# Moving the products K S and Q S of the next chunk behind the transposes of the tokens

## The chip, the cores and the metric

The kernel runs on one core of one Trainium2 chip. The metric is device time in microseconds (us) of one execution; six runs of the kernel before gave a median of 648.7 us (648.18 to 649.58). The engines are called PE (TensorE, the matrix products), DVE (VectorE), ACT (ScalarE), POOL (GpSimd) and SP (SyncE, which here only issues transfers).

## The reference

Two things are computed one after the other. First a delta-rule attention for 4 batches x 8 heads, 768 tokens, head size 48, then a feed-forward layer on its output (3072 tokens x 384, hidden width 2048), all in float32:

```python
k_n = k / (norm(k) + 1e-6)
for t in range(S):
    y[t]  = q[t] @ state                       # read before the update
    v_old = k_n[t] @ state
    state = state + beta[t] * outer(k_n[t], v[t] - v_old)
out = gelu(y_tokens @ w_in) @ w_out
```

## The kernel before

**Chunks.** The 768 tokens are cut into 12 chunks of 64. For a chunk c the loop over tokens becomes products: Gram blocks of the keys (`grams`), a triangular inverse, products with the state (`against_state`, L605: `K S` and `Q S`, 64 small products for each of the two units, a unit being two batches x 8 heads), the subtraction of the values (`subtract`, L626: L633 and L635 on DVE, a copy on ACT, L634), `solve` (L642), `outputs` (L696: `use`, the new state L684, the tokens x L694) and `turns` (L718: six 128x128 transposes of the tokens into the layer's layout, then one copy by ACT into `xT`). Chunks are joined in pairs for the triangular inverse: `eliminate_steps` (L431) makes 30 pairs of small DVE instructions (L455, L457) and four wide 32x32-block transposes on DVE (L443, L466, L470), among them `back(0)` (L466), which writes the tile `XM` that the first join products read.

**The layer.** From chunk 2 on both layers of the feed-forward part are done with seven products in place of eight (Winograd's form of Strassen's method). The first layer (`part_of_layer`, L836) is done in two blocks b = 0, 1; each block is eleven groups of eight 128x128 products in the order P1, P5, P6, P2, R22, R11, P7, P3, R12, P4, R21. Three of them are tied to DVE: P6 is followed on DVE by L869 and L898, and P7 may write the same bank only after both; P7 is followed by L877, which reads the block C22 out of the bank that P4 goes on writing, so **P4 waits for L877**. L888 reads the bank of P3 and R12 (tag `sq`). The second layer (`two`, L913) is seven groups of 16 products, 128x192 outputs: n = 1, 5, 2, 6, 4, 7, 3; the last one, n = 3, goes to `psV2`, and L951 reads it on DVE.

**Windows.** The program is a list of steps with due times in units of a chunk; the steps are traced in order of time. In what follows *window w* is the stretch from w to w + 1: PE does the layer of chunk w - 1, and between its groups the small products of chunk w. In an odd window they are: K S and Q S at w + 0.367, `solve` with the masked Gram (`queries`) at w + 0.59, `outputs` at w + 0.72, `turns` at w + 0.93. An even window also has the two Gram products and the three join steps of a pair, and K S and Q S at w + 0.465. Each run of small products is chained by `together` (L577), which fixes the order within the run. The elimination of a pair begins in the last third of an even window and fills the odd window after it.

**Who orders what.** DVE executes exactly in the order of the due times. For PE, ACT, POOL and SP a planner chooses the order by readiness, with the traced order as priority, except where a chain (`together`, `behind`, `keep`) fixes it.

**Banks.** PSUM holds two double banks with the tag `dn` (small products, `psX` of `turns`, `psV2`), two banks `mlp`, and one each with the tags `z` and `sq`. `psK` of the two units takes both `dn` tiles.

**Transposed queries.** `turned_q` (L363, instruction L365) makes `Qt` of chunk c on DVE from the tile `Qb`, which `load_blocks` (L123, issues at L134 on SP, 16 a chunk) fills. All chunks share `Qb` and `Qt`: `Qb` of chunk c can be loaded once `turned_q` of c - 1 has read it. Values: `load_v` (issues at L96) fills `V`, four tiles for two chunks, so the tiles of chunk c come free when `subtract` of chunk c - 2 has read them; POOL then scales `V` (L337).

Of the kernel before, what the change touches and what calls it, by code (L numbers as in the profile page):

```python
# [16 lines left out]
def kernel(  # L17
# [33 lines left out]
    NC = S // C  # L51
    NP = H // 2
    NA = B // 2
# [15 lines left out]
    def dn(name):  # L69
        return ps.tile([128, 2, 512], F32, tag="dn", name=name)  # L70

    def sq(name, *shape):
        return small[0].tile([128, *shape], F32, tag="sq", name=name)
# [17 lines left out]
    tiles = {}  # L91
# [513 lines left out]
    def against_state(us):  # L605

        for u in us:
            u.W = wk.tile([128, H, D], F32, tag="W", name="W")
            u.y = None
            if u.c == 0:  # L610
                nc.gpsimd.tensor_tensor(u.W, u.V,
                                        ng[:, u.a].unsqueeze(2).to_broadcast([128, H, D]),
                                        op=ALU.mult)
                continue
            u.psK = dn("psK")[:, :, 0:2 * NP * D].rearrange("q r (x j d) -> q x r j d", x=2, d=D)
            for x in range(2):
                for j in range(NP):
                    for r, p in QUADS:
                        rows = slice(r * C, r * C + D)
                        to = HALF[p ^ (j % 2)] if x and u.c > 1 else HALF[p]  # L620
                        nc.tensor.matmul(u.psK[to, x, r, j, :], lhsT=(u.Qt if x else u.Kt)[rows, p, j, :],  # L621
                                         rhs=St[rows, u.a, p ^ r, j, :], start=True, stop=True)
        if us[0].c != 2:
            subtract(us)

    def subtract(us):  # L626
# [100 lines left out]

    def state_steps(c, first=(), second=()):
        us = [tiles[c, a] for a in range(NA)]
        return [(together, (against_state, us), *first), (together, (solve, us), *second),  # L730
                (outputs, us), (together, (turns, us))]


    FH = NF // 2
# [1 line left out]
    DH = DM // 2  # L736
# [47 lines left out]
    W2 = {}  # L784
# [128 lines left out]
    def two(c, n):  # L913
        if n == 1:
            W2["X"] = ps.tile([128, 2, DH], F32, tag="mlp", name="psX2")
            W2["o"] = [wk.tile([128, DM], F32, tag="o_sb", name="o_sb") for a in range(NA)]
            product(W2["X"][:, 0], A[0][0], B11, True)
        elif n == 5:
            W2["Z"] = small[0].tile([128, DH], F32, tag="z", name="psZ2")
            product(W2["Z"], W2["S"], T[1], True)  # L920
            W2["p1"] = more[0].tile([128, DH], F32, tag="p1", name="p1")
            nc.scalar.copy(W2["p1"], W2["X"][:, 0])
        elif n == 6:
            W2["Y"] = ps.tile([128, 1, DH], F32, tag="mlp", name="psY2")
            product(W2["Y"][:, 0], A[0][0], T[2], True)
        elif n == 2:
            product(W2["X"][:, 0], A[0][1], B21, False)
        elif n == 7:
            product(W2["Y"][:, 0], A[1][0], T[3], False)
        elif n == 4:  # L930
            product(W2["X"][:, 1], A[1][1], T[4], True)
        else:
            W2["V"] = dn("psV2")[:, 0, 0:DH]
            product(W2["V"], A[0][1], B22, True)

    def read2(c, n):
# [47 lines left out]
    def at(first, last, steps):  # L984

        total, done, timed = sum(s[0] for s in steps), 0.0, []
        for w, *step in steps:
            timed.append((first + (last - first) * (done + 0.5 * w) / total, step))
            done += w
        return timed  # L990
# [120 lines left out]
    def state_at(c, *times, first=(), second=()):  # L1111

        steps = state_steps(c, first, second)
        if len(times) > len(steps):
            steps = steps[:-1] + [(turn, tiles[c, a]) for a in range(NA)]
        return [(t, step) for t, step in zip(times, steps) if t is not None]
# [27 lines left out]
    for c in range(4, NC):  # L1144
        us = [tiles[c, a] for a in range(NA)]
        t = {4: 1.8, 5: 2.1}.get(c, c - 2.9)
        plan += [at(t, t + 0.01, [(1.0, load_blocks, c, "Kb", k)])]
        t = 3.2 if c == 4 else c - (0.72 if c % 2 == 0 else 0.9)
        plan += [at(t, t + 0.01, [(1.0, load_blocks, c, "Qb", q)])]
        t = c - (2.1 if c % 2 == 0 else 2.62) if c > 5 else {4: 2.1, 5: 2.74}[c]  # L1150
        plan += [at(t, t + 0.01, [(1.0, load_k, c, "Kn")])]
        plan += [at(c - 0.4, c - 0.39, [(1.0, load_k, c, "Kp")])]
        t = {4: 2.7262, 5: 2.955}.get(c, c - (1.77 if c % 2 == 0 else 2.57))
        plan += [at(t, t + 0.0005, [(1.0, turned_k, u) for u in us])]
        t = c + (-0.12 if c % 2 == 0 else 0.23)
        plan += [at(t, t + 0.01, [(1.0, turned_q, u) for u in us])]
    def gram(c):
        return [(grams, [tiles[c, a] for a in range(NA)])] if c < NC else []

    def query(c):  # L1160
        return [(queries, [tiles[c, a] for a in range(NA)])]
# [13 lines left out]
    for c in range(2, NC):  # L1175
        for b in range(NB):
            t = c + 1.06 + 0.2576 * b
            plan += [at(t, t + 0.001, [(1.0, add_p5)])]
        plan += [at(c + 1.42, c + 1.421, [(1.0, mix, c, 1, 0)]),
                 at(c + 1.94, c + 1.941, [(1.0, read_x, c)]),  # L1180
                 at(c + 1.715, c + 1.716, [(1.0, mix, c, 3, h) for h in range(2)])]
    for w in range(3, NC):
        two_ahead = w + 2 < NC
        if w % 2:
            if w == 3:
                plan += [at(w + 0.09, w + 0.092, [(1.0, transposed, u, (1,)) for u in fourth]
                            + [(1.0, together, *gram(5))]),
                         at(w, w + 0.001, [(1.0, norms, 5), (1.0, prep, 5)]),
                         at(w + 0.1, w + 0.101, [(1.0, finish, 4)])]
                plan += rows_of(2, w, ((1, 0.102, 0.103), (2, 0.16, 0.2), (4, 0.224, 0.31),  # L1190
                                       (2, 0.325, 0.365), (1, 0.395, 0.4), (2, 0.485, 0.5),
                                       (2, 0.508, 0.54), (5, 0.6, 0.685), (7, 0.76, 0.88),
                                       (3, 1.0, 1.05), (5, 1.07, 1.1), (1, 1.11, 1.111),
                                       (1, 1.16, 1.161), (1, 1.166, 1.167)))
            elif two_ahead:
                plan += rows_of(w // 2 + 1, w, ((1, -0.35, -0.349), (1, -0.34, -0.339),
                                                (1, -0.23, -0.229), (5, -0.22, -0.14),
                                                (1, -0.07, -0.06), (3, 0.005, 0.05),
                                                (3, 0.068, 0.148), (2, 0.156, 0.215),
                                                (2, 0.235, 0.31), (3, 0.325, 0.365),  # L1200
                                                (1, 0.398, 0.409), (2, 0.485, 0.5),
                                                (1, 0.508, 0.54), (5, 0.6, 0.685),
                                                (3, 0.76, 0.8), (1, 1.003, 1.004),
                                                (1, 1.16, 1.161), (1, 1.166, 1.167)))
            plan += [state_at(w, w + 0.367, w + 0.59, w + 0.72, w + 0.93, second=query(w))]
        else:
            j0, j1, j2 = join_steps(w // 2)
            t = w + (0.25 if w == 4 else 0.165)
            plan += [at(t, t + 0.001, [(1.0, together, j0, *query(w))]),
                     at(w + 0.37, w + 0.371, [(1.0, together, j1, *gram(w + 2))]),  # L1210
                     state_at(w, w + 0.465, w + 0.58, w + 0.72, w + 0.93, second=[j2] + gram(w + 3))]
            plan += spread("join", 4, w + 0.395)
            plan += spread("join", 4, w + 0.64)
            if two_ahead:
                plan += spread("gram", 2, w + 0.375) + spread("gram", 2, w + 0.42)
                plan += spread("gram", 4, w + 0.63)
                plan += [at(w + 0.366, w + 0.367, [(1.0, norms, w + 2)]), at(w + 0.3715, w + 0.372, [(1.0, prep, w + 2)]),
                         at(w + 0.56, w + 0.561, [(1.0, norms, w + 3), (1.0, prep, w + 3)]),
                         at(w + 0.64, w + 0.641, [(1.0, finish, w + 2)])]
# [32 lines left out]
```

## Time and profile before

| | us |
|---|---|
| median of 6 runs | 648.7 |
| the profiled execution, its own time | 648.99 |
| its span (first to last instruction) | 647.3 |
| around the span | 1.69 |

Seen from the first group P1 of a window to the next P1, the profile gives:

| window | from, us | length | PE busy | DVE busy |
|---|---|---|---|---|
| 3 | 171.82 | 48.33 | 47.92 | 45.09 |
| 4 | 220.15 | 53.30 | 51.61 | 45.01 |
| 5 | 273.45 | 45.45 | 45.42 | 39.42 |
| 6 | 318.90 | 51.11 | 51.11 | 40.07 |
| 7 | 370.01 | 45.44 | 45.41 | 39.41 |
| 8 | 415.45 | 51.11 | 51.11 | 40.07 |
| 9 | 466.56 | 45.45 | 45.42 | 39.42 |
| 10 | 512.01 | 48.92 | 48.92 | 27.39 |
| 11 | 560.93 | 44.22 | 44.22 | 20.42 |

PE counts as busy while any product is in its pipeline, so a short wait between two groups hardly shows in this column. The surer reading is the distance between the starts of consecutive groups, which is constant where nothing waits. A line of the view by time has: start, duration, engine, line of the kernel, operation, output<-inputs, shapes, count, and in brackets the idle time before it with what ended it.

### The profile page before, as it was taken

The page shows a single profiled execution, that of the slowest core. Times are in us where ns is not written, and L with a number is a line of the kernel's source. Part 1 is how long each engine was busy: PE and PEld are TensorE (multiplying, and loading weights), DVE is VectorE, ACT ScalarE, POOL GpSimd, SP SyncE. Part 2 cuts the span into 40 slices and gives each one's busy share as a digit, 9 for nine tenths or more (in the row PEclk, how much of TensorE's full clock was granted, in tenths as well). Part 3 has the DMA queues.
Part 4 walks back from the last instruction along what each step waited for, and adds up shares of the span by engine and source line. Part 5 has one row for each costly group of instructions (what it writes and reads, how often), then busy time and mean ns, then how long its engine had stood idle before and what let it go on. Part 6 is the DMA issues. An engine that isn't in the chain of part 4 may idle for free.

```text
span 647.3 us, 22145 instructions
## 1 busy us (share of the span) xinstructions
PE 621.5 (96%) x9702; PEld 574.6 (89%) x9702; DVE 506.3 (78%) x1028; ACT 251.6 (39%) x578; POOL 64.1 (10%) x58
## 2 busy tenths in 40 slices
PE   6777999999999989999999999999999999999997
PEld 5666776776799989999999999999999999999997
DVE  6999999999899987999677999677999664354342
ACT  3366744615452247133157133157132153132230
POOL 4041400100311004001004001004001000000000
PEclk9976999999999999999999999999999999999999
DMA  9885645302432235321425321412211400100101
GB/s 129 180 269 173 125 137 158 47 4 57 75 59 44 55 36 89 54 35 31 69 30 90 55 31 33 71 18 40 46 27 33 70 5 3 25 2 2 26 2 25
DMA packets 158433, 39.79 MB, mean 61 GB/s; under 512 B 150016, under 2 KB 153216, under 8 KB 158336
## 3 DMA queue, kind: packets, MB, share of 16 engines
q1 hardware_dynamic: 155344, 36.94, 29.3%
q10 hardware_dynamic: 2992, 1.43, 1.0%
q8 instruction: 76, 1.25, 0.8%
q14 instruction: 21, 0.17, 0.1%
HBM read 33.62 MB, written 4.72 MB: 59 GB/s over the span
## 4 chain that ended last, share of the span: by engine, by line
PE 81%; DVE 13%; issue 2%; DMA 2%; ACT 1%; POOL 0%; SPq 0%; ACTq 0%; DVEq 0%; POOLq 0%
PE psX L791 12%; PE psY L846 11%; PE psX L846 8%; PE psY L791 7%; PE psV L846 5%; PE psZ L846 5%; PE psO L761 5%; PE psH L747 5%; PE psZ L791 4%; PE psV L791 4%; PE psK L621 3%; PE psG L375 3%; PE psJ L547 3%; DVE tmp L455 2%; DVE Nu L457 2%
## 5 line engine op out<-in xcount | busy, mean ns | idle before, releaser
L457 DVE TENSOR_TENSOR Nu<-Nu,tmp 128x30 f32<-128x30 f32 (+9 forms) x180 | 60.9, 338 | 6.2
L455 DVE TENSOR_TENSOR tmp<-Nu 128x30 f32<-128x30 f32 (+9 forms) x180 | 61.3, 340 | 4.7
L846 PE MATMUL psX<-xT,w_in_sb 128*128 128x128 f32 x480 | 64.6, 277 | 0.4 <-ACT pu L834 0.2
L846 PEld LDWEIGHTS psX<-xT,w_in_sb 128*128 128x128 f32 x480 | 58.8, 192 | 1.8 <-ACT pu L834 0.5
L834 ACT COPY xT<-psX 128x768 f32<-128x768 f32 x9 | 7.2, 799 | 124.3 <-PE psX L724 124.3
L791 PE MATMUL psX<-w_out_sb,G 128*128 128x192 f32 x320 | 55.3, 326 | 0.0
L312 POOL TENSOR_TENSOR n<-n,half 128x16 f32<-128x16 f32 x10 | 30.0, 3003 | 224.0 <-DVE n L310 203.8
L791 PEld LDWEIGHTS psX<-w_out_sb,G 128*128 128x128 f32 x320 | 52.1, 190 | 0.0
L747 PE MATMUL psH<-xT,w_in_sb 128*128 128x256 f32 x192 | 45.3, 389 | 2.0 <-ACT G L749 1.9
L761 PE MATMUL psO<-w_out_sb,G 128*128 128x384 f32 x128 | 44.5, 492 | 0.6 <-DVE w_out_sb L235 0.6
L747 PEld LDWEIGHTS psH<-xT,w_in_sb 128*128 128x128 f32 x192 | 36.1, 193 | 9.1 <-ACT G L749 3.4
L846 PE MATMUL psY<-xT,w_in_sb 128*128 128x128 f32 x320 | 42.3, 275 | 0.0
L846 PEld LDWEIGHTS psY<-xT,w_in_sb 128*128 128x128 f32 x320 | 39.0, 192 | 0.0
L834 ACT COPY pu<-psZ 128x512 f32<-128x512 f32 x40 | 23.4, 586 | 39.5 <-PE psZ L846 39.4
L761 PEld LDWEIGHTS psO<-w_out_sb,G 128*128 128x128 f32 x128 | 23.4, 190 | 14.9 <-DVE w_out_sb L235 1.6
L834 ACT ACTIVATE G<-G 128x512 f32<-128x512 f32 x40 | 25.2, 630 | 20.7 <-DVE G L877 19.9
L337 POOL TENSOR_TENSOR V<-V,n 128x384 f32<-128x384 f32 x18 | 16.5, 929 | 132.8 <-DMA V<-in_v_dram 78.4
L869 DVE TENSOR_TENSOR psY<-psY,pu 128x512 f32<-128x512 f32 x20 | 14.0, 698 | 19.0 <-PE psY L846 16.2
L791 PE MATMUL psY<-T,G 128*128 128x192 f32 x160 | 28.6, 332 | 0.0
L791 PE MATMUL psZ<-T,pu 128*128 128x192 f32 x160 | 28.6, 332 | 0.0
L791 PE MATMUL psV<-w_out_sb,G 128*128 128x192 f32 x160 | 27.7, 326 | 0.0
L791 PE MATMUL psX<-T,G 128*128 128x192 f32 x160 | 27.6, 326 | 0.0
(175 smaller groups left out, 1348.1 us busy)
## 6 DMA issues: line engine op xcount, KB each, us to landing
Kp<-in_k_dram SPq DMA_DIRECT2D x76, 96.0 KB, 3.3
w_out_sb<-in_moe_w_in_dram SPq DMA_DIRECT2D x24, 256.0 KB, 4.0
w_raw<-in_moe_w_out_dram SPq DMA_DIRECT2D x16, 384.0 KB, 4.4
V<-in_v_dram SPq DMA_DIRECT2D x48, 96.0 KB, 3.0
out_dram<-o_sb SPq DMA_DIRECT2D x36, 96.0 KB, 2.2
Qp<-in_q_dram SPq DMA_DIRECT2D x64, 32.0 KB, 2.1
Qp<-in_q_dram SPq DMA_DIRECT2D x16, 96.0 KB, 4.0
Qp<-in_k_dram SPq DMA_DIRECT2D x32, 32.0 KB, 2.2
```

The lines of the kernel that those rows point to most:

```text
L312: nc.gpsimd.tensor_tensor(flat, flat, half, op=ALU.pow)
L337: engine.tensor_tensor(u.V, u.V, ns[u.c][:, u.a].unsqueeze(2).to_broadcast([128, H, D]), op=ALU.mult)
L375: nc.tensor.matmul(psG[HALF[p], r, i * NP + j, :], lhsT=u.Kt[rows, p, j, :], rhs=(u.Qt if x else u.Kt)[rows, p, j, :], start=True, stop=True)
L455: nc.vector.tensor_tensor(tmp, nu[:, j + 1:, j:j + 1].to_broadcast([128, n, j]), nu[:, j:j + 1, 0:j].to_broadcast([128, n, j]), op=ALU.mult)
L457: nc.vector.tensor_tensor(nu[:, j + 1:, 0:j], nu[:, j + 1:, 0:j], tmp, op=ALU.add)
L547: nc.tensor.matmul(psJ[HALF[p], k, :], lhsT=(xm if level else off)[rows, us, :], rhs=zf[rows, us, HB:C] if level else xm[rows, us, :], sta ...
L621: nc.tensor.matmul(u.psK[to, x, r, j, :], lhsT=(u.Qt if x else u.Kt)[rows, p, j, :], rhs=St[rows, u.a, p ^ r, j, :], start=True, stop=True)
L747: nc.tensor.matmul(psH, lhsT=w_in_sb[:, f // 2, m, f % 2 * 128:(f % 2 + 1) * 128], rhs=xTs[c][:, m, :], start=(m == 0), stop=(m == NM - 1))
L761: nc.tensor.matmul(u.psO, lhsT=G[:, u.a, f, :], rhs=w_out_sb[:, f, :], start=(f == 0), stop=(f == NF - 1))
L791: nc.tensor.matmul(ps_, lhsT=lhs[:, f, :], rhs=rhs[:, f, :], start=first and f == 0, stop=f == FH - 1, skip_group_check=not first)
L834: tc.keep_in_program_order(fn(*args))
L846: nc.tensor.matmul(ps_[:, i], lhsT=lhs[:, f // 2, f % 2 * 128:(f % 2 + 1) * 128], rhs=rhs, start=first and i == 0, stop=True, skip_group_c ...
```

## The change

1. `against_state` of chunk c + 1, for c + 1 = 4 to 11, is traced in the same `together` run as `turns` of chunk c (due at c + 0.93), behind the transposes, and no longer as a run of its own inside window c + 1.
2. `subtract` of these chunks becomes a step of its own, due at c - 0.04: behind the differences of `xT` (`mix_x`, L816), ahead of L951.
3. `psV2`, the last product of the second layer, goes to the bank `sq` instead of a `dn` tile.
4. `turned_q` of an odd chunk moves from c + 0.23 to c - 0.12, where that of an even chunk already is; the loads of `Qb` move from c - 0.72 (even) and c - 0.9 (odd) to c - 1.1.
5. On DVE, in odd windows from 5 on, four elimination pairs come earlier. In window 4, `back(0)` moves from 4.11 to 4.153 (behind L877 of block 0, whose place is 4.1523), `back(1)` and `back(2)` from 4.16 and 4.166 to 4.2 and 4.201.

```diff
-        if us[0].c != 2:
+        if us[0].c in (1, 3):
             subtract(us)
...
     def state_steps(c, first=(), second=()):
         us = [tiles[c, a] for a in range(NA)]
+        after = [(against_state, [tiles[c + 1, a] for a in range(NA)])] if 2 < c < NC - 1 else []
         return [(together, (against_state, us), *first), (together, (solve, us), *second),
-                (outputs, us), (together, (turns, us))]
+                (outputs, us), (together, (turns, us), *after)]
...
-            W2["V"] = dn("psV2")[:, 0, 0:DH]
+            W2["V"] = sq("psV2", DH)
...
-        t = 3.2 if c == 4 else c - (0.72 if c % 2 == 0 else 0.9)
+        t = 3.2 if c == 4 else c - 1.1
         plan += [at(t, t + 0.01, [(1.0, load_blocks, c, "Qb", q)])]
...
-        t = c + (-0.12 if c % 2 == 0 else 0.23)
+        t = c - 0.12
         plan += [at(t, t + 0.01, [(1.0, turned_q, u) for u in us])]
...
+    plan += [at(c - 0.04, c - 0.0395, [(1.0, subtract, [tiles[c, a] for a in range(NA)])])
+             for c in range(4, NC)]
...
-                                       (3, 1.0, 1.05), (5, 1.07, 1.1), (1, 1.11, 1.111),
-                                       (1, 1.16, 1.161), (1, 1.166, 1.167)))
+                                       (3, 1.0, 1.05), (5, 1.07, 1.1), (1, 1.153, 1.154),
+                                       (1, 1.2, 1.201), (1, 1.201, 1.202)))
...
-                                                (2, 0.235, 0.31), (3, 0.325, 0.365),
-                                                (1, 0.398, 0.409), (2, 0.485, 0.5),
-                                                (1, 0.508, 0.54), (5, 0.6, 0.685),
-                                                (3, 0.76, 0.8), (1, 1.003, 1.004),
+                                                (2, 0.235, 0.31), (4, 0.325, 0.4),
+                                                (2, 0.43, 0.475), (2, 0.485, 0.5),
+                                                (1, 0.508, 0.54), (4, 0.6, 0.685),
+                                                (2, 0.76, 0.8), (1, 1.003, 1.004),
...
-            plan += [state_at(w, w + 0.367, w + 0.59, w + 0.72, w + 0.93, second=query(w))]
+            plan += [state_at(w, w + 0.367 if w == 3 else None, w + 0.59, w + 0.72, w + 0.93, second=query(w))]
...
-                     state_at(w, w + 0.465, w + 0.58, w + 0.72, w + 0.93, second=[j2] + gram(w + 3))]
+                     state_at(w, None, w + 0.58, w + 0.72, w + 0.93, second=[j2] + gram(w + 3))]
```

## The prediction

> **What bounds the kernel now.** First the page: engines' busy time, the slices of the span and the chain that ended last.
>
> ```profile
> PE 621.5 (96%) x9702; PEld 574.6 (89%) x9702; DVE 506.3 (78%) x1028; ACT 251.6 (39%) x578; POOL 64.1 (10%) x58
> PE   6777999999999989999999999999999999999997
> PEclk9976999999999999999999999999999999999999
> PE 81%; DVE 13%; issue 2%; DMA 2%; ACT 1%; POOL 0%; SPq 0%; ACTq 0%; DVEq 0%; POOLq 0%
> ```
>
> PE sets the end, at full clock from the fifth slice on. So a change pays only if it removes work from PE or a wait of PE. I therefore read PE by time, group by group. A group of eight 128x128 products takes 0.893 us where nothing waits, a group of 16 second-layer products 2.60.
>
> ```profile
> 383.41 1.06 PE L846 MATMUL psZ<-xT,w_in_sb 128*128 128x128 f32 x8
> 384.39 0.68 PE L621 MATMUL psK<-St,Kt 48*64 48x48 f32 x32
> ...
> 386.41 1.16 PE L846 MATMUL psX<-xT,w_in_sb 128*128 128x128 f32 x8
> 387.40 0.83 PE L846 MATMUL psY<-xT,w_in_sb 128*128 128x128 f32 x6
> ```
>
> Start to start: 0.98 for the group before K S and Q S (0.09 too long), 2.02 for their 128 products, 0.99 for the group after (0.10 too long). Together 2.20 us, of which two edges are 0.19.
>
> ```profile
> 364.15 2.76 PE L791 MATMUL psY<-w_out_sb,G 128*128 128x192 f32 x16
> 366.75 0.82 PE L724 MATMUL psX<-ident,x 128*128 128x128 f32 x6
> 367.41 2.77 PE L791 MATMUL psV<-w_out_sb,G 128*128 128x192 f32 x16
> 370.01 1.05 PE L846 MATMUL psX<-xT,w_in_sb 128*128 128x128 f32 x8
> ```
>
> Around the transposes the distances are 2.60, 0.66, 2.60: **this run has no edges to save**. Now the waits. From the first P1 of window 3 (171.82) to the end, groups stand further apart than their work and edges in two sorts of place (and 0.2 in window 3, at 181.63, which the change does not touch).
>
> ```profile
> 220.15 1.13 PE L846 MATMUL psX<-xT,w_in_sb 128*128 128x128 f32 x8 [0.17 <-DVE p L943]
> 227.53 1.06 PE L846 MATMUL psV<-xT,w_in_sb 128*128 128x128 f32 x8
> 230.28 1.16 PE L846 MATMUL psY<-TX,w_in_sb 128*128 128x128 f32 x8 [1.69 <-DVE G L877]
> ```
>
> At the start of window 4: 2.93 for the last product before 220.15, then 1.03 and 0.99 for P1 and P5 (0.57 lost), and R12 to P4 2.75 in place of 0.89, P4 0.10 long (1.96 lost): 2.53. In windows 5, 7 and 9, P4 of block 1 also waits for L877: 0.19 before it and 0.10 in it, 0.29 each, 0.87. All waits that the change could remove come to **3.4 us**. They come from DVE, which in its own view is busy without a break there:
>
> ```profile
> 218.46 1.30 DVE L365 STREAM_TRANSPOSE Qt<-Qp 128x512 f32<-128x512 f32 x2
> ...
> 227.60 2.08 DVE L466 STREAM_TRANSPOSE XM<-Nu 128x1024 f32<-128x1024 f32 x1
> 229.57 0.66 DVE L877 TENSOR_TENSOR G<-psY,pu 128x512 f32<-128x512 f32 x1
> ```
>
> **The moved run itself: 0.** Eight runs of 2.20 leave the windows and eight come back behind the transposes. The number of runs with edges stays; the edge between transposes and K S is not in the trace. Between none (L791 to L724) and 0.09 (L846 to K S) I take 0.09, since the form of K S decides; the other end would be worth 8 x 0.09 = 0.7. The Trainium skill, "TensorEngine Tiling (Array Packing)", Key Properties, says that every change of the tiling mode drains the engine: by it the edge is paid wherever the run stands, so the joining saves nothing.
>
> The second unit's `psK` now needs the `dn` tile that `psX` leaves. ACT copies it 413.05 to 413.85 after transposes that began at 412.20; the first unit's products would end at 412.85 + 0.09 + 0.97 = 413.91. A wait of 0 to 0.1, taken as 0; eight times 0.1 goes into the range. `psV2` in `sq`: P3 of the next layer needs L951 done, six groups (5.4 us) after P1 begins; hidden. With `subtract` before it L951 comes 2.1 later, still 3 us early.
>
> **Window 3 to 4: -1.0.** K S and Q S of chunk 4 now follow the transposes, which end at 217.21. `Qt` of its first unit is done on DVE at 218.46 + 0.69 = 219.15, because seven elimination pairs stand before it. K S starts at 217.30 and its first half takes 0.50; then PE waits 1.4 until 219.2; the rest (0.47 + 0.47 + 0.58) ends at 220.72, the last product at 223.42, and nine groups later P4 is due at 223.42 + 8.04 = 231.46. On DVE L877 ended at 230.23; it loses L466 ahead of it (1.97 start to start) and gains `subtract` (2.09: four instructions, 247.36 to 249.45 in window 4): 230.35 to 230.6. So P4 no longer waits, but stands 1.18 later than 230.28, and 2.20 is gone later in the window. `XM` is then ready at 232.6, its join due at 233.3: hidden. Net 1.18 - 2.20 = -1.02.
>
> **Windows 4 to 5, 6 to 7, 8 to 9: +0.3 each, +0.9.** Taken at 6 to 7. PE is 2.20 earlier there, so its transposes end at 365.20 and the first half of K S at 365.79. DVE before the transposes hangs on POOL's square roots, and these on L888, which stood behind the two `Kt` transposes and `subtract` (346.01); without that wait and those four it runs at 343.36, so DVE is 2.65 earlier: its fifth elimination pair ends at 365.2 and not at 367.87. Then `turned_q`, new here: first unit done at 365.9, so PE waits 0.15 to 0.2. The last product and P1 come 0.2 later than before (370.2). DVE between there and L877 of block 0 has -2.65 + 1.29 (`turned_q`) + 2.09 (`subtract`) = +0.73: L877 ends at 378.2, P4 is due at 378.24: level. Later `turned_q` is gone from this window (-1.2), so DVE waits for P6 of block 1 as before. From its L869 to L877 there were 6.75 us; `subtract` leaves: L877 ends at 388.3, while P4 is due at 390.08 - 2.20 + 0.19 = 388.07. It waits 0.3 and pays 0.10, where 0.29 was lost before: +0.1. At 10 to 11 and at the turns into even windows DVE has idle time listed ahead of the products; 0.
>
> **Queues: +0.3.** `Qb` of an even chunk is now loaded at the start of the odd window. What follows it on SP are the layer's outputs and the values:
>
> ```profile
> 380.34 9.67 SPq L134 DMA_DIRECT2D Qp<-in_q_dram  x16
> 390.12 2.74 SPq L96 DMA_DIRECT2D V<-in_v_dram  x4
> ```
>
> In window 7 the four loads of `V` wait for `subtract` and for the 16 issues (0.60 each); 3.6 us later POOL scales `V` at 393.75, and DVE stretches:
>
> ```profile
> 394.41 1.20 DVE L907 TENSOR_TENSOR G<-G 128x512 f32<-128x512 f32 x1
> 395.53 0.97 DVE L455 TENSOR_TENSOR tmp<-Nu 128x184 f32<-128x184 f32 x1
> ```
>
> L907 takes 0.69 and this L455 0.35 without POOL: 0.5 + 0.6 = 1.1 us, now behind the last critical L877. After the change the 16 issues start at 366, with four output issues among them (2.3): `V` goes out at 376 to 378, POOL works at 380 to 384. There DVE has 0.9 us to spare before L869 of block 1. I take 0.1 in each of windows 5, 7, 9; the ends are 0 and 1.1. The Trainium skill, "SBUF — State Buffer", Who interferes with whom, says that a DVE instruction with two SBUF inputs and a reading POOL instruction exclude each other for the whole instruction; with POOL's own 0.83 that estimate would be up to 1.7 a window, more than the 1.1 measured, and L869, with one input in PSUM, would be spared.
>
> **Sum.** 0 - 1.0 + 0.9 + 0.3 = +0.2. The profiled execution, span 647.3 and 1.69 around it, took 648.99, so 649.2; the median is 0.3 lower: **648.9**.
>
> **Rivals.**
> 1. *POOL meets DVE at the critical place* (slower). If `V` goes out a few microseconds earlier or later than worked out, that is, if POOL starts between 372 and 380 or after 383 and before 388 on the clock of window 7, every stretch reaches P4: 3 x 1.1 in place of 0.3, 651.9. For it: the 16 issues stand exactly ahead of `V`. Against: 0.9 us of slack. Chance 0.18.
> 2. *The planner breaks the run* (mostly slower). `together` fixes an order, not neighbourhood; at 174.50 to 176.87 transposes are already split around a P2 group. If part of the last product slips between the units' K S, each of eight breaks costs edges of 0.30 (0.11 + 0.10 + 0.09): 2.4, less some of the 2.0 of waits for `Qt` that it covers: 650.5. Chance 0.16.
> 3. *The waits for `Qt` are covered* (faster). If the last product goes ahead of K S as a whole in window 3, the 1.4 vanishes, and with the three 0.2 it is 2.0: 646.9; with P4 in the odd windows free as well (3 x 0.4) 645.7. For it: the last product has all it needs at 217. Against: K S is traced first, and `subtract` on DVE would then wait for it. Chance 0.24.
>
> That nothing comes of the change is inside the forecast's case, chance 0.42, own range 647.6 to 650.2 (the wait for `Qt` 0.5 longer or shorter in window 3, 0.2 in the others, the edge, the `dn` waits).
>
> **Chances.** A measurement tells 0.2%, 1.3 us, from no change: 647.4 and 650.0 are the bounds. Faster 0.24 (rival 3); within 0.42 (0.38 of the forecast, 0.04 of rival 2); slower 0.34 (0.18 + 0.12 + 0.04). The range for 8 in 10 reaches into rivals 1 and 3: 646.4 to 651.9.
>
> **What would show it.** Right: K S directly behind the transposes, a wait for `Qt` of about 1.4 in front of window 4 and below 0.5 at the next odd windows, none in front of even ones; P4 of window 4 without its 1.7; P4 of block 1 in windows 5, 7, 9 still 0.2 to 0.5 late. Wrong: L791 between the products of K S; L907 or L455 stretched before L877; or a wait of K S for ACT's copy of `psX` over 0.1.

## The result and the profile after

The change made the kernel slower: 650.32 us median (649.51 to 652.62) against 649.21 (648.18 to 650.66) for the kernel before, ratio **1.0027**, 95% interval 1.0019 to 1.0034, or 1.7 us. The profiled execution took 650.23, with a span of 648.5 (before: 648.99 and 647.3). Nine of the 17 executions took 649.5 to 650.3 and eight 651.3 to 652.6; the ratio goes by all of them (their mean is 650.92, that of the kernel before 649.17), and the profiled execution is one of the nine. The change adds a line, so that from L731 on line numbers are one higher (L791 is L792, L877 is L878); ks_back and ks_after_last, which drop that line, and the versions of the kernel before have the old ones.

From the page of the changed kernel, the busy time and the chain that ended last:

```profile
PE 621.7 (96%) x9702; PEld 574.4 (89%) x9702; DVE 503.6 (78%) x1028; ACT 252.2 (39%) x578; POOL 62.9 (10%) x58
...
PE 67%; DVE 21%; issue 5%; POOL 3%; DMA 2%; ACT 1%; SPq 0%; ACTq 0%; DVEq 0%; POOLq 0%
```

PE's busy time is the same, so no PE work went away. DVE does 2.7 us less and has 21% of the last chain where it had 13%: more of the end now goes through DVE.

The table that carries the rest sets each stretch between two `turns` of the tokens against the kernel before. Each stretch is read from the starts of PE's groups, and the last one runs to the end of PE's last product. The first stretch runs from the first P1 of window 3. No edit touches the part before it, which ends at 171.8 to 172.7 in all profiles but one (174.91 in ks_after_last, see there), so it is kept out. Windows 3 and 4 differ by 0.1 to 0.2 where nothing in them was changed (window 3 in xm_alone and bank_alone, window 4 of xm_odd against xm_alone), so a difference of that size there can be chance.

| difference from before, us | w3 | w4 | w5 | w6 | w7 | w8 | w9 | w10 to end | sum |
|---|---|---|---|---|---|---|---|---|---|
| length before | 44.73 | 53.64 | 45.44 | 51.11 | 45.44 | 51.11 | 45.44 | 134.42 | |
| the changed kernel | +0.11 | -0.95 | +0.53 | +0.02 | +0.55 | +0.03 | +0.69 | +0.04 | +1.02 |
| xm_alone | -0.13 | -1.23 | 0 | 0 | 0 | 0 | 0 | 0 | -1.36 |
| after_xm_back | -0.04 | +0.46 | +0.93 | +0.03 | +0.54 | +0.02 | +0.72 | +0.05 | +2.71 |
| ks_back | -0.18 | -1.31 | +0.81 | 0 | +0.83 | 0 | +0.77 | 0 | +0.92 |
| ks_after_last | -0.17 | -1.20 | +1.04 | 0 | +0.53 | 0 | +0.69 | 0 | +0.89 |
| qt_early | +0.20 | -1.00 | +0.24 | +0.78 | +0.24 | +0.78 | +0.23 | +0.04 | +1.51 |
| tq_alone | +0.04 | +0.21 | +0.82 | 0 | +0.82 | 0 | +0.82 | 0 | +2.71 |
| bank_alone | -0.14 | -0.04 | 0 | 0 | 0 | 0 | +0.01 | 0 | -0.17 |
| xm_odd | -0.13 | -1.36 | -0.29 | 0 | -0.29 | 0 | -0.29 | 0 | -2.36 |
| after_relief | -0.17 | -0.84 | -0.25 | +0.03 | -0.24 | +0.02 | -0.25 | +0.04 | -1.66 |
| after_both | +0.06 | -1.49 | -0.26 | +0.02 | -0.26 | +0.03 | -0.26 | +0.04 | -2.12 |
| xm_odd4 | -0.06 | -1.18 | -0.29 | 0 | -0.29 | 0 | -0.29 | 0 | -2.11 |

The changed kernel gains 0.84 in windows 3 and 4 and loses 1.77 in windows 5, 7 and 9; the even windows from 6 on, in which K S and Q S moved as well, do not change. Two places of its view by time follow. At the turn into window 4:

```profile
217.62 0.68 PE L621 MATMUL psK<-St,Kt 48*64 48x48 f32 x32
219.67 0.68 PE L621 MATMUL psK<-St,Qt 48*64 48x48 f32 x32 [1.37 <-DVE Qt L365]
```

2.05 us lie between the two starts, 0.50 where nothing waits: Q S stands 1.55 for `Qt`. In window 7, at block 1:

```profile
389.45 1.06 PE L847 MATMUL psV<-xT,w_in_sb 128*128 128x128 f32 x8
...
390.00 0.68 DVE L878 TENSOR_TENSOR G<-psY,pu 128x512 f32<-128x512 f32 x1
...
390.74 1.16 PE L847 MATMUL psY<-TX,w_in_sb 128*128 128x128 f32 x8 [0.23 <-DVE G L878]
```

P4 comes 1.29 after R12 in place of 0.89 and is 0.10 long: 0.50 lost, 0.29 before the change. At this turn Q S also stands 0.26 (it starts at 368.18, 0.76 after K S, in place of 0.50) and is 0.03 long behind the wait, and P4 of block 0 is 0.05 long. Window 7 adds up: 0.26 + 0.03 + 0.05 + (0.50 - 0.29) = 0.55. In window 9 P4 of block 0 is 0.10 late and 0.10 long; `turned_q` took 1.46 there in place of 1.31, for a reason that the trace does not show.

### The profile page after: what moved, and what is told of

Read it like the earlier page. It is cut to its first block, busy times and chain, and to the rows that moved or that the text cites. A ratio compares the mean times of both kernels' runs of the same rounds, so it can differ in the third digit from the quotient of the medians.

```text
span 648.5 us, 22137 instructions
## 1 busy us (share of the span) xinstructions
PE 621.7 (96%) x9702; PEld 574.4 (89%) x9702; DVE 503.6 (78%) x1028; ACT 252.2 (39%) x578; POOL 62.9 (10%) x58
## 4 chain that ended last, share of the span: by engine, by line
PE 67%; DVE 21%; issue 5%; POOL 3%; DMA 2%; ACT 1%; SPq 0%; ACTq 0%; DVEq 0%; POOLq 0%
PE psY L847 9%; PE psX L792 8%; PE psX L847 7%; PE psZ L847 5%; PE psY L792 5%; PE psO L762 5%; PE psH L748 5%; PE psV L792 4%; PE psV L847 4%; DVE tmp L455 3%; PE psK L621 3%; DVE Nu L457 3%; PE psZ L792 3%; POOL n L312 3%; PE psJ L547 2%
## 5 line engine op out<-in xcount | busy, mean ns | idle before, releaser
L457 DVE TENSOR_TENSOR Nu<-Nu,tmp 128x30 f32<-128x30 f32 (+9 forms) x180 | 60.3, 335 | 6.2
L455 DVE TENSOR_TENSOR tmp<-Nu 128x30 f32<-128x30 f32 (+9 forms) x180 | 60.2, 335 | 4.7
L792 PE MATMUL psX<-w_out_sb,G 128*128 128x192 f32 x320 | 55.3, 326 | 0.0
L792 PEld LDWEIGHTS psX<-w_out_sb,G 128*128 128x128 f32 x320 | 52.1, 190 | 0.0
L870 DVE TENSOR_TENSOR psY<-psY,pu 128x512 f32<-128x512 f32 x20 | 13.9, 697 | 21.9 <-PE psY L847 17.7
L792 PE MATMUL psZ<-T,pu 128*128 128x192 f32 x160 | 28.6, 332 | 0.0
L792 PE MATMUL psY<-T,G 128*128 128x192 f32 x160 | 28.6, 332 | 0.0
L792 PE MATMUL psV<-w_out_sb,G 128*128 128x192 f32 x160 | 28.5, 331 | 0.0
L792 PE MATMUL psX<-T,G 128*128 128x192 f32 x160 | 27.6, 326 | 0.0
L792 PE MATMUL psY<-w_out_sb,G 128*128 128x192 f32 x160 | 27.6, 326 | 0.0
```

Source lines behind the costliest of these rows:

```text
L455: nc.vector.tensor_tensor(tmp, nu[:, j + 1:, j:j + 1].to_broadcast([128, n, j]), nu[:, j:j + 1, 0:j].to_broadcast([128, n, j]), op=ALU.mult)
L457: nc.vector.tensor_tensor(nu[:, j + 1:, 0:j], nu[:, j + 1:, 0:j], tmp, op=ALU.add)
L792: nc.tensor.matmul(ps_, lhsT=lhs[:, f, :], rhs=rhs[:, f, :], start=first and f == 0, stop=f == FH - 1, skip_group_check=not first)
L870: nc.vector.tensor_tensor(L1["Y1"], L1["Y1"], L1["pu"][:, 0], op=ALU.add)
```

## The experiments

**Theory W**: the move of K S and Q S gives and costs nothing by itself; the time is set by PE's waits for DVE, whose order the change altered in several places, for better in window 4, for worse in the odd windows. Rivals: **M**, the gain and the loss come with the moved run itself; **E**, they come from the edges between small and full-size products.

### Window 4: which part gains?

**xm_alone** is the kernel before with only this:

```diff
-                                       (3, 1.0, 1.05), (5, 1.07, 1.1), (1, 1.11, 1.111),
-                                       (1, 1.16, 1.161), (1, 1.166, 1.167)))
+                                       (3, 1.0, 1.05), (5, 1.07, 1.1), (1, 1.153, 1.154),
+                                       (1, 1.2, 1.201), (1, 1.201, 1.202)))
```

> The kernel before, with only the change's reordering in window 4: back(0) behind L877 of block 0, back(1) and back(2) after it. Theory W (the changed kernel's time is set by the waits of PE for DVE; the move of K S and Q S itself costs and gives nothing): L877 no longer stands behind L466, so P4 of window 4 comes up to 1.96 us earlier. 1.7 to 1.9 us below the kernel before, ratio 0.9971 to 0.9974; the 0.57 us in front of P1 of window 4 stays. Rival M (the gain in window 4 comes from K S and Q S having left it, so that P4 is due later; the order on DVE is not what counts): within 0.3 us of before, with P4 still waiting over 1 us.

Measured: 0.9982 (0.9967 to 0.9997), window 4 1.23 us shorter. Its view by time:

```profile
227.94 0.65 DVE L877 TENSOR_TENSOR G<-psY,pu 128x512 f32<-128x512 f32 x1
...
228.51 2.12 DVE L466 STREAM_TRANSPOSE XM<-Nu 128x1024 f32<-128x1024 f32 x1
...
228.92 1.06 PE L846 MATMUL psY<-TX,w_in_sb 128*128 128x128 f32 x8
```

L877 is done ahead of L466 and P4 waits for nothing. The gain is smaller than expected by 0.5 to 0.7, since P6 of block 1 now comes 0.41 late (1.30 after the group at 233.96) and is 0.10 long, and the place in front of P1 lost 0.2 more than before. **after_xm_back** is the other half, the changed kernel with those two lines as they were.

> The changed kernel, with window 4's order on DVE as before the change: L466 (back(0)) ahead of L878 of block 0 again. In the changed kernel L878 runs 230.44 to 231.1 and P4 starts at 231.96. Theory W (window 4 gained by the order on DVE): L878 comes 1.97 us later, ends at 233.1, and P4 waits 1.1 us; 1.1 us above the changed kernel, ratio to the kernel before 1.0036 to 1.0054. Rival M (window 4 gained because K S and Q S went out from ahead of P4): as the changed kernel, 1.0019 to 1.0034, no wait at P4.

Measured: 1.0042 (1.0028 to 1.0055), window 4 1.41 us longer than in the changed kernel.

```profile
230.58 2.10 DVE L466 STREAM_TRANSPOSE XM<-Nu 128x1024 f32<-128x1024 f32 x1
232.54 0.70 DVE L878 TENSOR_TENSOR G<-psY,pu 128x512 f32<-128x512 f32 x1
...
233.29 1.16 PE L847 MATMUL psY<-TX,w_in_sb 128*128 128x128 f32 x8 [1.05 <-DVE G L878]
```

The wait is back, with K S gone from ahead of it. The four kernels form a square: in window 4 the order on DVE is worth -1.23 without the move and -1.41 with it, the move (and what comes with it) +0.46 without the new order and +0.28 with it. So W holds here and M falls: window 4 gained by the edit that has nothing to do with K S. after_xm_back also has window 5 at +0.93 in place of +0.53, for the reason shown under ks_after_last: POOL's second L337 (290.67) met a L455, 0.79 for 0.40, and P4 waited 0.40 longer.

### The odd windows: the run, or the order on DVE?

**ks_back** keeps the bank, `turned_q` and the loads, and the order of the pairs; items 1 and 2 of the change are undone, so K S, Q S and `subtract` stand where they stood in the kernel before.

> The changed kernel, with K S, Q S and subtract put back into the windows where they were; the bank of the last product, the earlier turned_q and Qb loads and the order of the eliminations stay changed. Theory W: the odd windows keep most of their loss, because turned_q stands ahead of the elimination there and four pairs are moved; window 4 has its 1.7 to 1.9 us gain. By following the durations 0.4 us above the changed kernel, 1.1 above the one before: ratio 1.0010 to 1.0035, with P4 of block 0 or 1 in windows 5, 7 and 9 waiting 0.5 us or more. Rival M (the loss comes with the K S run: its edges and its wait): the loss goes and the gain of window 4 stays, 1.5 us or more below the kernel before, ratio below 0.9977.

Measured: 1.0014 (1.0005 to 1.0023). The odd windows lose 0.77 to 0.83 **without** the moved run, more than with it; window 4 keeps 1.31. The second half of M falls too. The difference between ks_back and the changed kernel is what items 1 and 2 do: +0.65 in windows 3 and 4, where K S now stands ahead of `Qt`, -0.64 in windows 5, 7 and 9, +0.09 in the rest, +0.10 in sum. So W's claim that the move by itself gives and costs nothing holds for the sum, not for each place. **tq_alone** asks which edit does it, the kernel before with only

```diff
-        t = 3.2 if c == 4 else c - (0.72 if c % 2 == 0 else 0.9)
+        t = 3.2 if c == 4 else c - 1.1
...
-        t = c + (-0.12 if c % 2 == 0 else 0.23)
+        t = c - 0.12
```

> The kernel before, with only item 4 of the change: turned_q of the odd chunks at c - 0.12 and the earlier loads of Qb; K S, Q S and the eliminations stay. The runs so far: with K S put back but the rest of the change kept, windows 5, 7 and 9 lost 0.8 us each, with PE waiting for L943, for L877 of block 0 and for L877 of block 1; window 4 kept its gain. Theory W (the odd windows lose because 1.29 us of turned_q stand ahead of DVE's critical instructions, which were level with PE before): with DVE 1.29 us later at L943 and L877 of block 0 and no pair moved to relieve it, P1, P4 and what follows wait 0.5 to 1.3 us a window, 1.5 to 3.9 in three: ratio 1.0023 to 1.0060, window 4 as before. Rival (the moved pairs are what costs): within 0.5 us of before, ratio 0.9992 to 1.0008.

Measured: 1.0040 (1.0028 to 1.0052), 0.82 in each of windows 5, 7 and 9 and nothing elsewhere but 0.2 at window 4. PE in window 7:

```profile
371.13 1.05 PE L846 MATMUL psX<-xT,w_in_sb 128*128 128x128 f32 x8
372.30 1.16 PE L846 MATMUL psZ<-TX,Sw 128*128 128x128 f32 x8
...
378.76 1.06 PE L846 MATMUL psV<-xT,w_in_sb 128*128 128x128 f32 x8
379.88 1.16 PE L846 MATMUL psY<-TX,w_in_sb 128*128 128x128 f32 x8
```

P1 to P5 takes 1.17 in place of 0.89, R12 to P4 1.12, and P5, P7 (376.88) and P4 are 0.10 long each (379.88 to 380.87 is 0.99). `turned_q` ends its 1.29 us on DVE just ahead of L943, and what follows was level with PE. So item 4 alone makes the loss of the odd windows, and the moved pairs, its rival, add nothing: ks_back has them and loses 0.77 to 0.83. Item 4 also moves the loads of `Qb`, and no run moves `turned_q` without them. In window 7 of this trace the loads cost nothing that shows: DVE has no idle time in front of `turned_q` (369.00), and POOL scales `V` at 393.25, behind the last L877 (391.47). In the changed kernel, with K S and `subtract` out of the window, the loss is 0.53 to 0.69 in place of 0.82.

**bank_alone** is the kernel before with `W2["V"] = sq("psV2", DH)`.

> The kernel before, with only item 3: the last product of the second layer in the bank sq. Theory W: nothing waits for it, L951 reads the bank six groups before P3 writes it again, and the dn tile that comes free was not waited for: within 0.3 us, ratio 0.9992 to 1.0008, every window as long as before. Rival (the bank costs or gives, by the read of L888 that must come first or by the free dn tile): a window longer or shorter by over 0.1 us, eight times that in all, over 0.8 us.

Measured: 1.0002 (0.9993 to 1.0010), every window from 5 on as long as before to 0.01.

### The edges, and the waits for Qt

**ks_after_last** puts the run one place later:

```diff
-        after = [(against_state, [tiles[c + 1, a] for a in range(NA)])] if 2 < c < NC - 1 else []
...
-                (outputs, us), (together, (turns, us), *after)]
+                (outputs, us), (together, (turns, us))]
...
-    plan += [at(c - 0.04, c - 0.0395, [(1.0, subtract, [tiles[c, a] for a in range(NA)])])
+    plan += [at(c - 0.03, c - 0.0299, [(1.0, together, (against_state, [tiles[c, a] for a in range(NA)]))])
+             for c in range(4, NC)]
+    plan += [at(c - 0.025, c - 0.0249, [(1.0, subtract, [tiles[c, a] for a in range(NA)])])
```

> The changed kernel, with K S and Q S of the next chunk one place later: behind the last product of the second layer, not directly behind the transposes; subtract is due right after. Theory W: the last product (2.6 us) covers the waits for Qt, which were 1.5 us into window 4 and 0.25 into windows 5, 7 and 9; P4 in the odd windows stays late, since subtract comes later as well. By following each engine's durations by hand 0.7 us below the changed kernel, at most 2.2: ratio to the kernel before 0.9990 to 1.0018. Rival E (what costs is the number of edges between small and full-size products, and standing behind the transposes saves one): eight edges of 0.09 to 0.19 more, so 0.7 to 1.5 us above the changed kernel: ratio 1.0037 to 1.0050.

Measured: 1.0011 (1.0001 to 1.0022). E falls: windows 6 and 8 have 51.11 here, 51.11 before and 51.13 in the changed kernel, with K S in three different places. The distances say why. Changed kernel, then ks_after_last:

```profile
412.66 0.82 PE L724 MATMUL psX<-ident,x 128*128 128x128 f32 x6
413.41 0.68 PE L621 MATMUL psK<-St,Kt 48*64 48x48 f32 x32
```

```profile
415.47 0.82 PE L724 MATMUL psX<-ident,x 128*128 128x128 f32 x6
416.13 2.77 PE L791 MATMUL psV<-w_out_sb,G 128*128 128x192 f32 x16
```

The transposes take 0.75 ahead of K S and 0.66 ahead of the last product; the 0.09 is then paid between the last product and K S (2.69 for 2.60), and the 0.10 behind K S by P1. The Trainium skill, "TensorEngine Tiling (Array Packing)", Key Properties, has every change of the tiling mode drain the engine, and these runs agree: the same two edges of 0.09 and 0.10 wherever the run stands. The 0.10 by itself would not show a drain, since a group behind a mere wait is as much too long (last section).

But the waits for `Qt` are all gone here and the kernel still loses 0.89 in the windows, 0.13 less than the changed one where W expected 0.7 (by the ratios 1.0 less, but their intervals touch). The odd windows lose the same 0.53 and 0.69, now all at P4: DVE reaches L877 when it did, and PE waits for it there and not at Q S. Window 5 shows one thing more:

```profile
291.87 1.09 POOL L337 TENSOR_TENSOR V<-V,n 128x384 f32<-128x384 f32 x1 [0.49 <-DMA V<-in_v_dram]
...
292.31 0.92 DVE L457 TENSOR_TENSOR Nu<-Nu,tmp 128x238 f32<-128x238 f32 x1
...
296.46 0.71 PE L846 MATMUL psY<-TX,w_in_sb 128*128 128x128 f32 x4 [0.75 <-DVE G L877]
```

POOL's scaling of `V` falls between L898 and L877 of block 1, one L457 takes 0.92 for 0.41, and P4 waits 0.91 where it waits 0.40 in window 7: the 0.51 arrives whole. That is rival 1 of the prediction, caught in a neighbour of the change. Without it the windows would lose 0.38 by an estimate, 0.64 less than the changed kernel, close to the 0.7 that W expected; 0.53 of that lies in windows 3 and 4, and nearly none in the odd windows.

The profiled execution of ks_after_last took 652.97, 2.7 above the median of its runs. Most of the excess stands ahead of window 3, in eight second-layer products of an early chunk that no edit touches. Changed kernel, then ks_after_last, then the clock of ks_after_last:

```profile
165.97 2.85 PE L762 MATMUL psO<-w_out_sb,G 128*128 128x384 f32 x8
```

```profile
167.15 4.54 PE L761 MATMUL psO<-w_out_sb,G 128*128 128x384 f32 x8
```

```profile
PEclk9985999999899999999999999999999999999999
```

The eleventh digit, the slice from 163 to 179 us, has a lower granted clock (0.79 on average from 165 to 173, 1.00 in the changed kernel), and the eight products take 1.69 us longer. So the time of an execution can move by that much without any window of the table moving.

**qt_early** has `turned_q` at c - 0.25 (3.74 for chunk 4), else as the changed kernel.

> The changed kernel, with turned_q of every chunk earlier on DVE (c - 0.25, for chunk 4 at 3.74), so that Qt is there when the transposes end. Theory W: no wait between the two halves of K S into windows 4, 5, 7 and 9, which were 1.5 and three times 0.25 us. What DVE does ahead is now 1.29 us later, and the waits of P7 and P4 behind it take back part: 0.7 us below the changed kernel by following the durations, at most 2.2; ratio to the kernel before 0.9990 to 1.0018. Rival (the wait between the halves is not Qt but ACT's copy out of the psX tile or the bank of the last product): the gap of 1.5 stays, time as that of the changed kernel, 1.0027.

Measured: 1.0017 (1.0007 to 1.0027), and 1.51 in the windows. The gap at Q S is gone, so it was `Qt`. But:

```profile
363.29 1.30 DVE L365 STREAM_TRANSPOSE Qt<-Qp 128x512 f32<-128x512 f32 x2
364.52 0.32 DVE L941 TENSOR_TENSOR o_sb<-psY,p 128x192 f32<-128x192 f32 x1
...
364.89 2.87 PE L792 MATMUL psY<-w_out_sb,G 128*128 128x192 f32 x16 [0.49 <-DVE o_sb L941]
```

L941 frees the bank of the next product, and 1.29 us of `turned_q` ahead of it cost 0.65 there (3.25 from the start of the product before, 361.64, in place of 2.60) and 0.10 behind it, at each turn into an odd window; it is counted in the even windows, +0.78, while the odd ones fall to +0.24. Together a pair of windows loses more than in the changed kernel, 1.02 against 0.58. In the windows the expected 0.7 of gain did not come; 0.49 more is lost. By the ratios it did, 0.65, but their intervals overlap. By the trace W was right on the wait and wrong on its balance.

### Versions that give DVE room

**xm_odd** is xm_alone and, in the odd windows, one pair from ahead of L877 of block 1 to behind it, in the kernel before:

```diff
-                                                (1, 0.398, 0.409), (2, 0.485, 0.5),
+                                                (1, 0.43, 0.44), (2, 0.485, 0.5),
```

> The kernel before, with window 4's reordering (which alone took 1.4 us out of the windows in the trace) and, in windows 5, 7 and 9, one elimination pair taken from ahead of L877 of block 1 to behind it. Theory W: the pair takes 0.8 us on DVE, P4 of block 1 waits 0.29 us in these windows, so all of it goes: 3 x 0.29 = 0.9 more, 2.2 us below before in all; ratio 0.9960 to 0.9975. Rival (those 0.29 us are not from DVE's order but from a transfer or from the bank itself): as with window 4 alone, 0.998.

Measured: 0.9966 (0.9954 to 0.9978), and exactly 0.29 in each of the three windows. **after_relief** gives DVE room in the changed kernel, with three pairs a window:

```diff
-                                                (1, -0.23, -0.229), (5, -0.22, -0.14),
-                                                (1, -0.07, -0.06), (3, 0.005, 0.05),
-                                                (3, 0.068, 0.148), (2, 0.156, 0.215),
-                                                (2, 0.235, 0.31), (4, 0.325, 0.4),
-                                                (2, 0.43, 0.475), (2, 0.485, 0.5),
+                                                (1, -0.23, -0.229), (4, -0.22, -0.14),
+                                                (2, -0.07, -0.06), (3, 0.005, 0.05),
+                                                (2, 0.068, 0.148), (2, 0.156, 0.215),
+                                                (2, 0.235, 0.31), (3, 0.325, 0.4),
+                                                (3, 0.43, 0.475), (3, 0.485, 0.5),
```

> The changed kernel, with the elimination pairs of windows 5, 7 and 9 set out anew: one from ahead of turned_q to behind it, one from ahead of L878 of block 0 and one from between L899 and L878 of block 1 to behind that L878. Nothing else. Theory W: the wait for Qt (0.25), P4 of block 0 (0.05 to 0.2) and P4 of block 1 (0.50) go, 0.8 us in each of three windows: 2.4 us below the changed kernel, ratio to the kernel before 0.998 to 1.0. Rival (the odd windows lose to the moved K S run itself, by its edges, its bank or its loads): as the changed kernel, 1.0027.

Measured: 0.9988 (0.9980 to 0.9997). The loss of the odd windows turns into a gain of 0.25, 2.5 us in three of them, with the moved run still in place:

```profile
388.37 1.06 PE L847 MATMUL psV<-xT,w_in_sb 128*128 128x128 f32 x8
389.27 1.06 PE L847 MATMUL psY<-TX,w_in_sb 128*128 128x128 f32 x8
```

P4 follows R12 in 0.90. The ratios of the two kernels differ by the same 2.5 us. The one long wait left is that for `Qt` of chunk 4. **after_both** takes it away as well:

```diff
-                                       (2, 0.508, 0.54), (5, 0.6, 0.685), (7, 0.76, 0.88),
-                                       (3, 1.0, 1.05), (5, 1.07, 1.1), (1, 1.153, 1.154),
+                                       (2, 0.508, 0.54), (5, 0.6, 0.685), (5, 0.76, 0.88),
+                                       (4, 1.0, 1.05), (3, 1.07, 1.1), (3, 1.1525, 1.1528), (1, 1.153, 1.154),
```

> The changed kernel with the odd windows set out anew as in the run before (which lost no time there and was left with one wait, 1.6 us for Qt of chunk 4), and in addition two elimination pairs of window 3 from ahead of turned_q to behind it and the last two from ahead of L878 of block 0 to behind it. Theory W: turned_q ends 1.56 us earlier, the wait goes; the end of the elimination, and with it XM, is not earlier, so the first join, 1.5 us earlier on PE, waits about 0.5 for it. 0.9 to 1.5 us below the run before, ratio to the kernel before 0.9960 to 0.9980. Rival (the wait is not DVE's place of turned_q but the load of Qb): the 1.6 us stay, 0.9988.

Measured: 0.9964 (0.9951 to 0.9977); in the windows 0.46 below after_relief, less than expected; by the ratios it would be 1.6.

```profile
233.03 1.15 PE L547 MATMUL psJ<-XM,G 32*64 32x64 f32 x32 [0.41 <-DVE XM L466]
```

Q S now follows K S in 0.51 (217.89 and 218.40). Of the 1.6 us, 0.57 come back in front of the join (1.46 from the group before it in place of 0.89), and 0.54 in block 1, behind the group at 236.20. **xm_odd4** does to xm_odd the same with one pair at each place.

> The kernel before with window 4 and the odd windows eased on DVE alone (ratio 0.9966 so far), and in addition one elimination pair of window 3 from ahead of L943 to behind it and the last one from ahead of L877 of block 0 to behind it. Theory W: L943 comes 0.78 us earlier, so the wait of 0.5 us in front of P1 of window 4 goes; the first join may wait up to 0.3 for XM. 0.2 to 0.5 us below, ratio 0.9957 to 0.9965, the shortest of all. Rival (P1 waits for something else there, the outputs' transfers or the bank): as without it, 0.9966.

Measured: 0.9955 (0.9940 to 0.9969). The trace does not bear out a gain over xm_odd: P1 no longer waits, but P7 does, 0.41 for L898 by the view by time and 0.57 by its distance, and the windows are 0.25 longer. The intervals of the two overlap; they can't be told apart. With them and after_both there are three versions some 0.35 to 0.45% below the kernel before, two of which do not move K S at all.

## Where the prediction held and where it failed, point by point

The forecast was +0.2, or 648.9, and the likeliest outcome (0.42) a change too small to tell. Measured are +1.7 and a median of 650.32, which the prediction's own bounds call slower (0.34). The median lies inside the range of 646.4 to 651.9 and outside the forecast's own 647.6 to 650.2. The range was that wide for the sake of rivals 1 and 3, and the profile shows neither, so it is luck that it holds.

- **The moved run itself, 0: right.** Joined to the transposes, before the last product or behind it, it has the same edges; the open one is 0.09, as taken. The even windows show 0.02 to 0.03 for ACT's copy of `psX`, inside the 0 to 0.1 given. The bank: 0.
- **Window 3 to 4, -1.0: right in size,** -0.84 with the stretch ahead of it. The wait for `Qt` is 1.55 (1.4 forecast), L878 is done 0.8 ahead of P4. after_xm_back confirms the step that loses L466 ahead of L877.
- **Windows 4 to 5, 6 to 7, 8 to 9, +0.9: the step that failed.** The mechanism was right and the size was not: +1.77. In window 7 the wait for `Qt` is 0.26 and not 0.15 to 0.2; L878 of block 0 was put level with P4, which was taken as free: it ends 0.12 ahead of P4 (379.67 + 0.68 against 380.47), and P4 is still 0.05 long (window 9: 0.20 lost); L870 to L878 of block 1 takes 4.75 where 6.75 less 2.09 was reckoned, and P4 loses 0.50 where 0.40 was forecast. Twice DVE was a tenth later than the sum of its durations, once level was not early enough, and the step had no slack to hide it. tq_alone shows how near it stood: `turned_q` put there alone costs 0.82 a window.
- **Queues, +0.3: 0 in this profile.** POOL began at 383.66 (381.4 by the clock of the forecast, whose P1 of window 7 stood 2.2 earlier), within the times forecast, and stretched one instruction of DVE:

```profile
383.66 0.83 POOL L337 TENSOR_TENSOR V<-V,n 128x384 f32<-128x384 f32 x1 [28.32 <-DMA V<-in_v_dram]
...
383.83 0.92 DVE L457 TENSOR_TENSOR Nu<-Nu,tmp 128x240 f32<-128x240 f32 x1
...
385.25 0.70 DVE L870 TENSOR_TENSOR psY<-psY,pu 128x512 f32<-128x512 f32 x1 [0.50 <-PE psY L847]
```

  0.51 longer, and behind it 0.50 us in which DVE waits for PE anyway: hidden, as argued.
- **Rival 1** did not happen in the profile of the changed kernel, by luck. In window 5 POOL's second instruction ends 0.03 ahead of the first L455 (289.54) of the stretch between L899 and L878:

```profile
288.68 0.83 POOL L337 TENSOR_TENSOR V<-V,n 128x384 f32<-128x384 f32 x1 [0.27 <-DMA V<-in_v_dram]
```

  In after_xm_back it came 0.56 later, counted from L870, and cost 0.40, in ks_after_last 0.51. **Rival 2**, a run broken by the planner, did not happen. **Rival 3** was wrong in its price: covered waits for `Qt` were to give 2.0 to 3.2; ks_after_last, which is that case, gave 0.13 in the windows (0.64 without POOL's meeting), qt_early lost 0.5 and even after_both kept 0.46 of 1.6. DVE hands the same lateness on to the next product that needs it.

So the difference was +1.7 where +0.2 was forecast. Of these 1.5, the windows hold 0.8: 0.9 more in the odd ones, 0.2 more in window 4, 0.1 for the copies of `psX` and the like, 0.3 less for the queues. The rest lies outside them: 0.2 ahead of window 3 in the profile, and 0.5 between the profiled executions, which differ by 1.24, and the ratio, whose interval says 1.2 to 2.2. These 0.5 come from which execution was profiled: that of the changed kernel lies 0.69 below the mean of all its executions, that of the kernel before 0.18 below its own. What made eight of the 17 longer is not shown, since none of them was profiled; a lower granted clock ahead of window 3 or a meeting of POOL, both seen in ks_after_last, could be it.

## What to carry to other kernels

When PE sets the end and a second engine runs level with it, removing a wait of PE moves most of it to the next product that needs that engine, unless an instruction that is not due is taken from ahead of the one that is: one elimination pair behind the critical read gave 0.29 us a window, exactly the wait. A change of several edits should be split before it is judged: here one reordering gave 1.2 to 1.4 us, one moved transpose cost 0.8 a window, and the edit that named the change came to 0.1 in sum. Where two engines are level to a tenth of a microsecond, a forecast should be put on the late side.

## What the runs showed of the hardware

- One POOL instruction of 0.83 us lengthened one DVE instruction with two SBUF inputs by 0.39 to 0.51 (L455 0.79 for 0.40, L457 0.92 for 0.41), while L870, with one input in PSUM, took its 0.70 beside the second L337 (384.96 to 385.79). The Trainium skill, "SBUF — State Buffer", Who interferes with whom, has such pairs exclude each other for the whole instruction. By it L457 would have ended at 384.49 + 0.41 = 384.90 in the changed kernel, an estimate; it ended at 384.75. So the direction and the exemption of PSUM agree, and the size is smaller by 0.15 here and by 0.14 in after_xm_back (291.76 for 290.67 + 0.83 + 0.40); the profile's spans on POOL are rough.
- A group of eight products that had to wait for DVE took 0.99 in place of 0.89 (379.88 to 380.87 in tq_alone, 390.74 to 391.73 in the changed kernel), also where its start was late by only 0.01 (376.88 to 377.87 in tq_alone): the wait cost 0.10 beyond its length. In the changed kernel the weight load of the first product then begins with the product, at 390.74; in the group before, which did not wait, it begins 0.11 ahead (389.34 and 389.45). Where P4 started on time, 0.12 behind the end of L878, half of the 0.10 was lost (380.47 to 381.41).
